# Twelve transfers of v for eight heads in place of 24 for four

## The chip, the cores and the metric

The kernel runs on one core of a Trainium2 chip. A core has five engines that each work through a queue of their own in order: TensorE (PE; its weight loads are shown apart as PEld), VectorE (DVE), ScalarE (ACT), GpSimd (POOL) and SyncE (SP). Sixteen DMA engines move data between the chip's memory and the core's; transfers are issued from the queues of SP, POOL and ACT. The metric is the device time of one execution in microseconds, as the median of several runs.

## The reference

Attention with a decaying state over blocks of 64 rows, and a two-layer network behind it. With B = 4, H = 8, S = 768, D = 64, and a factor `lam` for each head:

```python
for b in range(nb):                       # nb = 768 // 64
    sl = slice(b * block, (b + 1) * block)
    qb, kb, vb = q[:, :, sl], k[:, :, sl], v[:, :, sl]
    intra = einsum('bhic,bhjc->bhij', qb, kb) * Dmask
    intra = einsum('bhij,bhjd->bhid', intra, vb)
    inter = einsum('bhid,bhde->bhie', qb * lam_pow, kv_state)
    out[:, :, sl] = intra + inter
    kv_state = lam_block * kv_state + einsum('bhsd,bhse->bhde', kb * rev_pow, vb)

x = out.transpose(0, 2, 1, 3).reshape(B * S, H * D)      # 3072 x 512
h = x @ w_in                                             # 512 -> 2048
y = (maximum(h, 0) + alpha * minimum(h, 0)) @ w_out      # 2048 -> 512
```

So v is read twice in each block: in the product with the masked scores (`intra`) and in the product that brings the state on (`kv_state`).

## The kernel before

The work is cut into 24 units. Unit n stands for `units[n] = (c, bi, hh)`: c counts six chunks, bi the two batches of a chunk, hh the four heads 0 to 3 or 4 to 7. Chunk c has 256 rows of the sequence (`W`), that is four blocks of 64. Units 2m and 2m + 1 are therefore the two halves of the heads of one batch and the same rows.

A unit's q and k come as fp32 by `load` (L82), which takes eight heads or, with `half`, four, from SP or, with `"G"`, from POOL. `cast` (L257) makes fp16 of them; `turned` (L299, a transposing DMA from SP) or `turn` and `turn_copy` (L309, L323, over PE) bring them with the head's axis on the partitions; `key_decayed` and `decayed` scale them. Its v comes as fp16 by `load_v16` (L268), which POOL issues, since the transfer turns fp32 into fp16 on its way. The 24 transfers go into tiles of `kv_pool`, which has eight for the tag `v16`; the ninth transfer takes the first one's tile, once PE has read it for the last time, and so on.

Then PE works on the unit: `score_products` (L370, in L377), `inter` (L354, in L361) for the part that comes from the state, `intra` (L395, in L402) with v's halves as weights, and `state_products` (L415, in L422; for the first chunks under `state_in`, L466) with v against the decayed k. DVE masks the scores (`masked`, L388) and brings the state on (`states`, L457). `attended` (L431) copies the result as fp16 to `XT[c]`.

The four units of a chunk give one operand of the network: `up` (L493, in L498) for 16 slices of w_in, `relu` on ACT and `prelu` on DVE for the slope, and `down` (L530, in L534) for the first chunk. For later chunks the second product, and for the last two also the first, is done by a scheme with seven products of quarter matrices in place of eight; its sums (`w_sum`, `in_sum`, `g_sum`, `x_sum`) run on DVE and POOL in L573 and L576, and its products on PE in L655 and L780. `load_win` (L97) and `load_wout` (L103) bring the weights, also from POOL and also from fp32 to fp16.

All instructions of an engine are issued in the order of the calls that are written out from L799 to L1866, so the place of a `load_v16` call among the calls that use POOL sets when it is issued, and its place among the calls of POOL and SP what else the DMA engines have been given before it. Waits between engines, on landings and on tiles that are still being read are added from the data that each instruction reads and writes. `gate` (L111) holds SP until a piece of w_in or w_out has landed.

The places that matter below: L820 (unit 1), L833 (0), L836 (2), L841 (3), L889 (4), L941 (5), L1006 and L1007 (7 and 6), L1014 (8), L1103 (9), L1121 (13), L1137 (12), L1161 (10), L1187 (14), L1222 (11), L1261 (19), and from L1329 to L1477 the units 15, 16, 20, 17, 23, 18, 22, 21.

Of the kernel before, what the change touches and what calls it, by code (L numbers as in the profile page):

```python
# [11 lines left out]
def kernel(  # L12
# [19 lines left out]
    fp16 = mybir.dt.float16  # L32
# [4 lines left out]
    B, H, S, D = q.shape  # L37
    assert (B, H, S, D) == (4, 8, 768, 64)
    L = 128
    W = 2 * L  # L40
# [10 lines left out]
    kv_pool = ctx.enter_context(tc.tile_pool(name="kvh", bufs=8))  # L51
# [30 lines left out]
    def load(c, bi, x, half=None, queue="S"):  # L82

        pb, b = c // 2, 2 * (c % 2) + bi
        if (c, bi, x) not in raws:
            raws[c, bi, x] = raw_pool.tile([128, H, 2 * D], fp32, tag=f"{x}raw", name=f"{x}raw")
        heads = ds(0, H) if half is None else ds(4 * half, 4)
        i = "kqv".index(x)
        (nc.gpsimd if queue == "G" else nc.sync).dma_start(
            out=raws[c, bi, x][:, heads, :],  # L90
            in_=(k, q, v)[i][b, heads, ds(pb * W, W), :].rearrange("h (p e) d -> p h (e d)", e=2),
        )
# [4 lines left out]
    def load_win(i):  # L97
        nc.gpsimd.dma_start(
            out=w_in_sb[:, :, ts(i, 512)],
            in_=moe_w_in[:, ts(i, 512)].rearrange("(g p) f -> p g f", p=128),  # L100
        )

    def load_wout(i):  # L103
        nc.gpsimd.dma_start(
            out=w_out_sb[:, ts(i, 4), :],
            in_=moe_w_out[ts(i, 512), :].rearrange("(f p) d -> p f d", p=128),
        )
# [45 lines left out]
    for half in range(2):  # L153
# [7 lines left out]
        out=drop, in0=rel_i, scalar1=0.0, scalar2=-1e30, op0=ALU.is_lt, op1=ALU.mult  # L161
# [42 lines left out]
    def decay_mask(hp):  # L204
        m = dmask[:, hp // 2, :, hp % 2]
        nc.scalar.activation(m, m, AF.Exp)
# [34 lines left out]
    T = {}  # L241
# [3 lines left out]
    def copy_on(eng, out, in_):  # L245
        if eng == "A":
            nc.scalar.activation(out, in_, AF.Copy)  # L247
        elif eng == "V":
            nc.vector.tensor_copy(out=out, in_=in_)
        else:  # L250
            nc.gpsimd.tensor_copy(out=out, in_=in_)  # L251
# [16 lines left out]
    def load_v16(n):  # L268

        c, bi, hh = units[n]  # L270
        v16 = kv_pool.tile([128, 4, 2, D], fp16, tag="v16", name="v16")
        nc.gpsimd.dma_start(  # L272
            out=v16.rearrange("p h e d -> p h (e d)"),
            in_=v[2 * (c % 2) + bi, ds(4 * hh, 4), ds((c // 2) * W, W), :].rearrange("h (p e) d -> p h (e d)", e=2),
        )
        T.setdefault(n, {})["v16"] = v16

    def engine(x):
        return nc.gpsimd if x == "G" else nc.vector
# [29 lines left out]
    def turn(n, xs):  # L309

        t = T[n]
        tp = bank_pool.tile([128, len(xs), 2, 2, L], fp16, tag="bank", name="tp")
        for i, x in enumerate(xs):
            for e in range(2):
                for hp in range(2):
                    nc.tensor.transpose(  # L316
                        tp[:, i, e, hp, :],
                        t["qk16"][:, x, e, ds(2 * hp, 2)].rearrange("p l d -> p (l d)"),
                        ident,
                    )  # L320
        t["tp", xs] = tp

    def turn_copy(n, xs, eng):  # L323

        t = T[n]
        if "qkT" not in t:
            t["qkT"] = qkt_pool.tile([128, 2, 2, 2, L], fp16, tag="qkT", name="qkT")
        tp = t["tp", xs]
        if len(xs) == 1:
            copy_on(eng, t["qkT"][:, xs[0]], tp[:, 0])  # L330
        else:
            copy_on(eng, t["qkT"], tp)
        if xs[0] == 0:
            t["qps"] = tp[:, 0]
# [50 lines left out]
    def masked(n):  # L385
        t = T[n]
        t["sm"] = sm_pool.tile([128, 2, 2, 2, L], fp16, tag="sm", name="sm")
        nc.vector.tensor_tensor(  # L388
            out=t["sm"].rearrange("p a h x j -> p (a h) x j"),
            in0=t["s"].rearrange("p a h x j -> p (a h) x j"),  # L390
            in1=mask_of(units[n][2]),
            op=ALU.mult,
        )
# [37 lines left out]
    def attended(n, *how):  # L431
        co, bo, ho = units[n]
        if co not in XT:
            pool, tag = (raw_pool, "kraw") if co == 5 else (xt_pool, "xT")
            XT[co] = pool.tile([128, NHP, 2, 2, L], fp16, tag=tag, name="xT")
        x = XT[co][:, ds(2 * ho, 2), :, bo, :].rearrange("p h e (a j) -> p a (h e) j", a=2)
        o = acc[:, :, 0:256].rearrange("p a (he j) -> p a he j", j=64)
        if len(how) == 2:
            x, o = x[:, how[0]], o[:, how[0]]
        copy_on(how[-1], x, o)  # L440
# [52 lines left out]
    def up(c, f, bi=None):  # L493
        h = HP[c, f, bi] = bank_of("h_ps")
        n = CH if bi is None else W
        for gi in range(NHP):
            x = XT[c][:, gi]
            nc.tensor.matmul(  # L498
                h[:, 0:n] if bi is None else h[:, 0:n].rearrange("p (e j) -> p e j", e=2),
                lhsT=w_in_sb[:, gi, ts(f, 128)],  # L500
                rhs=x.rearrange("p e b j -> p (e b j)") if bi is None else x[:, :, bi, :],
                start=(gi == 0),
                stop=(gi == NHP - 1),
            )
# [3 lines left out]
    def relu(c, f, bi=None):  # L508
        n = CH if bi is None else W
        m = M[c, f, bi] = m_pool.tile([128, CH], fp32, tag="m", name="m")  # L510
        nc.scalar.activation(m[:, 0:n], HP[c, f, bi][:, 0:n], AF.Relu, scale=-1.0)  # L511

    def prelu(c, f, eng="V"):
        prelu_of(c, f, None, eng)
# [302 lines left out]
    cast(1, "k16", "V")  # L817
    tick(56)
    load(0, 1, "q", 1, "G")
    load_v16(1)  # L820
    decay_mask(1)
    cast(1, "q16", "A")
    mask_logs(3)
# [6 lines left out]
    query_decay(0, 0)  # L830
    load_alpha()
    load(0, 1, "k", 1, "G")
    load_v16(0)  # L833
    turn(1, (0,))
    turn_copy(1, (0,), "V")
    load_v16(2)  # L836
# [1 line left out]
    turn_copy(0, (1,), "V")  # L838
    turn(0, (0,))
    turn_copy(0, (0,), "A")  # L840
    load_v16(3)  # L841
    load_win(1)
    slopes_turn()
    slopes()
# [93 lines left out]
    prelu(0, 15)  # L938
    cast(4, "k16", "G")
    turn(4, (1,))  # L940
    load_v16(5)  # L941
    load_wout(1)
    up(0, 0)
    prelu(0, 14)
# [58 lines left out]
    w_sum(1, 3)  # L1003
    in_sum(1, 2)
    turn(7, (0,))
    load_v16(7)  # L1006
    load_v16(6)  # L1007
    first_state(5)
    down(0, 2, 1)
# [90 lines left out]
    down(0, 1, 2)  # L1100
    down(0, 1, 3)
    attended(6, "A")
    load_v16(9)  # L1103
    up(1, 14)
    cast(10, "q16", "G")
    load(3, 0, "k", None)
# [11 lines left out]
    gpsimd_waits(8)  # L1118
    key_decayed(9)
    masked(8)  # L1120
    load_v16(13)  # L1121
    cast(9, "k16", "A")
    down_copy(0, 1)
    relu(1, 14)
# [9 lines left out]
    prelu(1, 0)  # L1134
    relu(1, 8)
    prelu(1, 8)
    load_v16(12)  # L1137
    relu(1, 11)
    up(1, 7)
    prelu(1, 11)  # L1140
# [17 lines left out]
    masked(9)  # L1158
    prelu(1, 5)
    turned(10)  # L1160
    load_v16(10)  # L1161
    up(1, 12)
    relu(1, 13)
    relu(1, 12)
# [54 lines left out]
    load(4, 0, "k", None)  # L1219
    g_sum(1, 2, 0, 1)  # L1220
    g_sum(1, 3, 0, 0)
    load_v16(11)  # L1222
    second(1, 5, 1)
    g_sum(1, 3, 1, 0)
    states(10, (0, 1))
# [32 lines left out]
    masked(11)  # L1258
    cast(14, "k16", "A")
    cast(16, "k16", "G")  # L1260
    load_v16(19)  # L1261
    second(1, 7, 0)
    second(1, 3, 0)
    second(1, 7, 1)
# [61 lines left out]
    prelu(2, 12)  # L1326
    turned(15)
    second(1, 4, 1)
    load_v16(15)  # L1329
    load_v16(16)  # L1330
    states(14, (0, 1))
    up(2, 13)
    load_v16(20)
    relu(2, 5)
    masked(14)
    second_out(1, 4)
# [9 lines left out]
    prelu(2, 5)  # L1346
    in_sum(2, 2, "G")
    score_products(15)
    load_v16(17)
    prelu(2, 13)  # L1350
    cast(18, "q16", "A")
    turned(17)
# [6 lines left out]
    relu(2, 10)  # L1359
    cast(18, "k16", "A")  # L1360
    key_decayed(19)
    load_v16(23)
    up(2, 9)
    attended(14, "A")
    prelu(2, 10)
# [9 lines left out]
    inter(15)  # L1375
    relu(2, 6)
    load(5, 1, "q")
    load_v16(18)
    relu(2, 9)
    cast(19, "k16", "A")  # L1380
    score_products(16)
# [25 lines left out]
    up(3, 10)  # L1407
    relu(2, 7)
    relu(3, 8)
    attended(16, "A")  # L1410
    up(3, 1)
    prelu(2, 7)
# [28 lines left out]
    cast(20, "q16", "G")  # L1441
    relu(3, 3)
    intra(18)
    load_v16(22)
    score_products(19)
    cast(21, "k16", "A")
    cast(22, "k16", "A")
# [26 lines left out]
    turned(22)  # L1474
    g_sum(2, 3, 1, 1, "G")
    turned(21)
    load_v16(21)  # L1477
    score_products(20)
    state_products(20)
    g_sum(2, 3, 0, 0)  # L1480
# [416 lines left out]
```

## Time and profile before

| | |
|---|---|
| median of three runs | 201.76 us (201.7 to 206.57) |
| the profiled execution | 201.59 us |
| its span | 199.8 us, mean granted TensorE clock 0.999 |
| read from and written to the chip's memory | 27.27 MB and 6.29 MB |
| transfers issued from POOL (q0) | 17,776 packets, 10.23 MB |
| transfers issued from SP (q1) | 41,236 packets, 19.87 MB |
| transfers of v | 24, 128 KB each as they arrive; median 5.5 us from issue to landing |

The span runs from the first to the last instruction of the program; the time of the execution has 1.8 us more around it. The page gives the busy time of each engine, the span in 40 slices of 5 us, the chain of work that ended last, the costliest groups of instructions, and the issues of the DMA queues. In a row of the timeline the columns are the start in us, the time taken in us, the engine, the line, the operation with the names of what it writes and reads, their shapes, and how many instructions the row merges; in brackets stands how long the engine stood idle before and what ended that. An issue on POOL or SP is the making of the transfer's list alone; the data move later, and a transfer has landed when its last byte has been confirmed.

### The profile page before, as it was taken

How to read it: one execution, taken by the hardware profiler on the slowest of the kernel's cores; microseconds unless marked ns; L12 is line 12 of the kernel's file. 1: busy time of each engine (PE TensorE's matmuls, PEld its weight loads, DVE VectorE, ACT ScalarE, POOL GpSimd, SP SyncE). 2: the span in 40 equal slices, each digit the busy share in tenths (PEclk: the TensorE clock that was granted, in tenths of full speed). 3: DMA queues.
4: the chain of work that ended last, by engine and by line, in shares of the span. 5: the costliest groups of instructions: out<-in, count | busy, mean ns of one | idle time of the engine just before them, and what ended most of it. 6: DMA issues, size and time to landing. Idle time of an engine off the chain costs nothing.

```text
span 199.8 us, 5865 instructions
## 1 busy us (share of the span) xinstructions
PE 193.7 (97%) x2351; PEld 129.1 (65%) x2351; DVE 172.7 (86%) x320; ACT 130.9 (66%) x281; POOL 143.0 (72%) x161
## 2 busy tenths in 40 slices
PE   7999999999999999999999999999999999999992
PEld 7875454546545688666557767666666666788891
DVE  6988789999899999899999997899989999895800
ACT  5895775337967898697769589364686986633022
POOL 8999859964999649999999889850575213556700
PEclk9999999999999999999999999999999999999999
DMA  5999999999999989999996925120040001113143
GB/s 165 283 194 216 255 268 232 204 251 295 231 147 265 264 148 242 196 276 130 273 210 147 172 30 152 41 76 0 2 157 3 2 0 54 56 41 117 55 145 118
DMA packets 59199, 30.53 MB, mean 153 GB/s; under 512 B 29652, under 2 KB 57956, under 8 KB 59172
## 3 DMA queue, kind: packets, MB, share of 16 engines
q1 hardware_dynamic: 41236, 19.87, 41.0%
q0 software_dynamic: 17776, 10.23, 34.4%
q8 instruction: 18, 0.29, 0.6%
q14 instruction: 9, 0.07, 0.1%
q10 hardware_dynamic: 160, 0.07, 0.1%
HBM read 27.27 MB, written 6.29 MB: 168 GB/s over the span
## 4 chain that ended last, share of the span: by engine, by line
PE 84%; DVE 10%; ACT 3%; issue 1%; ACTq 0%; DVEq 0%
PE h_ps L498 27%; PE y L655 16%; PE b L655 12%; PE b L780 5%; PE o_ps L534 4%; PE acc L402 4%; PE s L377 3%; PE a L780 3%; PE e L780 3%; DVE sm L388 2%; PE acc L361 2%; PE tp L316 2%; DVE dmask L195 1%; PE acc L422 1%; DVE t L573 1%; ACT xT L247 1%
## 5 line engine op out<-in xcount | busy, mean ns | idle before, releaser
L498 PE MATMUL h_ps<-xT,w_in_sb 128*128 128x512 f16 (+1 forms) x264 | 59.5, 373 | 0.0
L655 PEld LDWEIGHTS <-g 128*128 128x128 f16 x464 | 44.7, 98 | 10.1 <-DVE g L573 0.6
L526 DVE SCALAR_TENSOR_TENSOR g<-m,oma,h_ps 128x512 f16<-128x512 f32 (+1 forms) x66 | 45.7, 725 | 3.6 <-ACT m L511 3.0
L511 ACT ACTIVATE m<-h_ps 128x512 f32<-128x512 f32 (+1 forms) x66 | 37.4, 582 | 15.6 <-PE h_ps L498 14.6
L498 PEld LDWEIGHTS <-w_in_sb 128*128 128x128 f16 x264 | 24.3, 98 | 25.4 <-DMA w_in_sb<-in_moe_w_in_dram 0.9
L388 DVE TENSOR_TENSOR sm<-s,dmask 128x1024 f16<-128x1024 f32 x24 | 29.2, 1217 | 1.7 <-PE s L377 1.7
L655 PE MATMUL y<-w_out_sb,g 128*128 128x256 f16 x224 | 27.9, 273 | 0.3 <-DVE g L573 0.3
L573 POOL TENSOR_TENSOR g<-g 128x512 f16<-128x512 f16 x11 | 13.2, 1204 | 16.3 <-DVE s L576 16.3
L341 POOL TENSOR_TENSOR qdT<-qkT,qdecay 128x512 f16<-128x512 f16 (+1 forms) x20 | 20.9, 1050 | 0.0
L655 PE MATMUL b<-t,g 128*128 128x256 f16 x160 | 19.8, 273 | 0.0
L247 ACT ACTIVATE xT<-acc 128x512 f16<-128x512 f32 x22 | 13.1, 595 | 9.4 <-PE acc L422 5.6
L272 POOL DMA_DIRECT2D v<-in_v_dram x24 | 18.8, 788 | 0.0
L457 DVE SCALAR_TENSOR_TENSOR R<-R,rdecay,acc 128x128 f16<-128x128 f16 x54 | 15.5, 341 | 2.8 <-ACT xT L247 2.2
L573 POOL TENSOR_TENSOR g<-g,g 128x512 f16<-128x512 f16 x12 | 14.3, 1206 | 5.0 <-DVE g L573 2.9
L576 POOL TENSOR_TENSOR s<-g,g 128x512 f16<-128x512 f16 x9 | 10.4, 1156 | 8.4 <-DVE g L526 8.4
L534 PE MATMUL o_ps<-w_out_sb,g 128*128 128x512 f16 x64 | 15.3, 379 | 0.0
L247 ACT ACTIVATE o_sb<-y 128x512 f32<-128x512 f32 (+2 forms) x12 | 6.2, 526 | 13.1 <-PE y L697 7.1
L290 ACT ACTIVATE kdec<-kraw,kdecay 128x64 f16<-128x64 f32 x56 | 14.0, 342 | 0.0
L292 POOL TENSOR_TENSOR kdec<-kraw,kdecay 128x512 f16<-128x512 f32 x13 | 13.6, 1054 | 0.4 <-DVE qdT L341 0.4
L251 POOL CAST qk<-kraw 128x512 f16<-128x512 f32 x10 | 6.5, 654 | 5.0 <-DMA kraw<-in_k_dram 5.0
L377 PE MATMUL s<-qkT 64*64 64x128 f16 x384 | 9.9, 219 | 0.2
L402 PE MATMUL acc<-sm,v 64*64 64x128 f16 x384 | 9.9, 220 | 0.2
(130 smaller groups left out, 369.3 us busy)
## 6 DMA issues: line engine op xcount, KB each, us to landing
out_dram<-o_sb SPq DMA_DIRECT2D x23, 256.0 KB, 2.5
kraw<-in_k_dram SPq DMA_DIRECT2D x7, 512.0 KB, 6.8
qraw<-in_q_dram SPq DMA_DIRECT2D x6, 512.0 KB, 6.1
v<-in_v_dram POOLq DMA_DIRECT2D x24, 128.0 KB, 5.5
w_in_sb<-in_moe_w_in_dram POOLq DMA_DIRECT2D x4, 512.0 KB, 7.8
w_out_sb<-in_moe_w_out_dram POOLq DMA_DIRECT2D x4, 512.0 KB, 9.7
qraw<-in_q_dram POOLq DMA_DIRECT2D x6, 256.0 KB, 6.9
qraw<-in_q_dram SPq DMA_DIRECT2D x6, 256.0 KB, 6.3
```

The lines of the kernel that those rows point to most:

```text
L247: nc.scalar.activation(out, in_, AF.Copy)
L272: nc.gpsimd.dma_start(out=v16.rearrange("p h e d -> p h (e d)"), in_=v[2 * (c % 2) + bi, ds(4 * hh, 4), ds((c // 2) * W, W), :].rearrange( ...
L341: engine(eng).tensor_tensor(out=qdT[:, :, :, p], in0=(t["qps"] if eng == "P" else t["qkT"][:, 0])[:, :, :, p], in1=qdecay[:, hh, :, :, p], ...
L388: nc.vector.tensor_tensor(out=t["sm"].rearrange("p a h x j -> p (a h) x j"), in0=t["s"].rearrange("p a h x j -> p (a h) x j"), in1=mask_of ...
L402: nc.tensor.matmul(ot[a][ds(hl * 64, 64), hp, :], lhsT=t["v16"][p, 2 * hp + hl, e, :], rhs=t["sm"][p, hl, hp, 1 - e, :], start=(2 * pb + a ...
L498: nc.tensor.matmul(h[:, 0:n] if bi is None else h[:, 0:n].rearrange("p (e j) -> p e j", e=2), lhsT=w_in_sb[:, gi, ts(f, 128)], rhs=x.rearr ...
L511: nc.scalar.activation(m[:, 0:n], HP[c, f, bi][:, 0:n], AF.Relu, scale=-1.0)
L526: engine(eng).scalar_tensor_tensor(out=g, in0=m, scalar=oma[:, f : f + 1], in1=h, op0=ALU.mult, op1=ALU.add)
L534: nc.tensor.matmul(O[c, t], lhsT=g_of(c, f)[:, t // 2, t % 2, :], rhs=w_out_sb[:, f, :], start=(f == 0), stop=(f == NF - 1),)
L573: engine(eng).tensor_tensor(out=out, in0=a, in1=b, op=ALU.subtract)
L655: nc.tensor.matmul(Y[c, k][:, ds(b * HALF, HALF)], lhsT=left(c, i, f, b), rhs=right(i, f), start=(f == 0 and b == 0 and i in (1, 5)), stop ...
L780: nc.tensor.matmul(t, lhsT=w, rhs=x, start=(g == 0 and i in (1, 5)), stop=(g == 1), skip_group_check=True)
```

## The change

`load_v16` brings all eight heads of a batch, that is two units, in one transfer into a tile twice as large. There are four such tiles in place of eight, so they take the same room. Both units get their half of the tile as a slice. Each of the twelve calls that stay brings units n and n + 1; the fourth pair before gives its tile. The other calls, their order, the engines and the explicit waits are as before. The diff, with the moved calls and little of what is around them:

```diff
@@ -268,12 +268,13 @@
     def load_v16(n):
 
         c, bi, hh = units[n]
-        v16 = kv_pool.tile([128, 4, 2, D], fp16, tag="v16", name="v16")
+        pair = kv_pool.tile([128, H, 2, D], fp16, tag="v16", name="v16", bufs=4)
         nc.gpsimd.dma_start(
-            out=v16.rearrange("p h e d -> p h (e d)"),
-            in_=v[2 * (c % 2) + bi, ds(4 * hh, 4), ds((c // 2) * W, W), :].rearrange("h (p e) d -> p h (e d)", e=2),
+            out=pair.rearrange("p h e d -> p h (e d)"),
+            in_=v[2 * (c % 2) + bi, :, ds((c // 2) * W, W), :].rearrange("h (p e) d -> p h (e d)", e=2),
         )
-        T.setdefault(n, {})["v16"] = v16
+        for m in (n - hh, n - hh + 1):
+            T.setdefault(m, {})["v16"] = pair[:, ds(4 * (m - n + hh), 4)]
@@ -817,7 +818,7 @@
     load(0, 1, "q", 1, "G")
-    load_v16(1)
+    load_v16(0)
     decay_mask(1)
@@ -830,7 +831,6 @@
     load(0, 1, "k", 1, "G")
-    load_v16(0)
     turn(1, (0,))
     turn_copy(1, (0,), "V")
     load_v16(2)
@@ -838,7 +838,6 @@
     turn_copy(0, (0,), "A")
-    load_v16(3)
     load_win(1)
@@ -938,7 +937,6 @@
     turn(4, (1,))
-    load_v16(5)
     load_wout(1)
@@ -1003,7 +1001,6 @@
     turn(7, (0,))
-    load_v16(7)
     load_v16(6)
@@ -1100,7 +1097,6 @@
     attended(6, "A")
-    load_v16(9)
@@ -1118,7 +1114,7 @@
     masked(8)
-    load_v16(13)
+    load_v16(10)
@@ -1134,7 +1130,6 @@
     prelu(1, 8)
-    load_v16(12)
@@ -1158,7 +1153,7 @@
     turned(10)
-    load_v16(10)
+    load_v16(12)
@@ -1219,7 +1214,6 @@
     g_sum(1, 3, 0, 0)
-    load_v16(11)
@@ -1258,7 +1252,7 @@
     cast(16, "k16", "G")
-    load_v16(19)
+    load_v16(16)
@@ -1326,11 +1320,9 @@
     second(1, 4, 1)
-    load_v16(15)
-    load_v16(16)
+    load_v16(18)
     states(14, (0, 1))
     up(2, 13)
-    load_v16(20)
@@ -1346,7 +1338,6 @@
     score_products(15)
-    load_v16(17)
@@ -1359,7 +1350,7 @@
     key_decayed(19)
-    load_v16(23)
+    load_v16(20)
@@ -1375,7 +1366,6 @@
     load(5, 1, "q")
-    load_v16(18)
@@ -1407,6 +1397,7 @@
     relu(3, 8)
+    load_v16(22)
     attended(16, "A")
@@ -1441,7 +1432,6 @@
     intra(18)
-    load_v16(22)
@@ -1474,7 +1464,6 @@
     turned(21)
-    load_v16(21)
```

The calls for 4 (L889), 8 (L1014) and 14 (L1187) stay where they are and bring 4/5, 8/9 and 14/15.

## The prediction

> **What bounds the kernel now.** I read the page first: the span, the busy shares, the chain and the strip of DMA slices.
>
> ```profile
> span 199.8 us, 5865 instructions
> PE 193.7 (97%) x2351; PEld 129.1 (65%) x2351; DVE 172.7 (86%) x320; ACT 130.9 (66%) x281; POOL 143.0 (72%) x161
> DMA  5999999999999989999996925120040001113143
> PE 84%; DVE 10%; ACT 3%; issue 1%; ACTq 0%; DVEq 0%
> ```
>
> TensorE (PE) works in 97% of the span and 84% of the chain that ended last is PE; GpSimd (POOL), whose queue the change shortens, does not stand in that chain at all. PE takes its instructions in order, so whatever stops it early moves everything behind it. The DMA engines are full (digit 9) from the second slice to about 110 us (slices are 5 us). So the question is less what POOL saves than when each half of v lands against the PE instruction that first needs it.
>
> Next, the waits and POOL's groups kept apart by shape, with the page's list of DMA issues.
>
> ```profile
> PEld L316 <- POOL qk L251: 0.3, 1, 0.3
> PEld L655 <- POOL g L573: 0.2, 1, 0.2
> ...
> POOL g L573 <- DVE s L576: 16.3, 3, 8.1
> ```
> ```profile
> L272 POOL DMA_DIRECT2D v<-in_v_dram x24 | 18.8, 788 | 0.0
> L89 POOL DMA_DIRECT2D qraw<-in_q_dram x6 | 4.6, 761 | 0.6 <-DMA w_in_sb<-in_moe_w_in_dram 0.6
> L98 POOL DMA_DIRECT2D w_in_sb<-in_moe_w_in_dram x4 | 3.1, 767 | 0.0
> ```
> ```profile
> v<-in_v_dram POOLq DMA_DIRECT2D x24, 128.0 KB, 5.5
> w_in_sb<-in_moe_w_in_dram POOLq DMA_DIRECT2D x4, 512.0 KB, 7.8
> ```
>
> PE and its weight loads wait 0.3 + 0.2 = 0.5 us for POOL in the whole run. An issue on POOL costs about 0.78 us whether it brings 128 KB (788 ns) or 512 KB (767 ns), so bytes do not set it. All of these transfers, however, have the same number of pieces by the code: 128 partitions times four (four heads of v or q, four groups of w_in). No row has 128 times eight.
>
> **The change part by part.** *Twelve issues less.* The ends for an issue of eight heads are 0.79 us (one issue, as bytes do not matter) and 2 x 0.79 = 1.58 us (two, if pieces set it). POOL thus saves between 24 x 0.788 - 12 x 0.79 = 9.4 us and nothing. No row lies nearer to either, so I take the middle, 1.2 us an issue and 4.5 us saved. Its worth on the path is near zero: POOL is not in the chain, and its longest wait, 16.3 us, is for VectorE (DVE). If all PE waits for POOL went, that would be the 0.5 us above. Nothing below rests on the issue's price, unless it is far above 1.58 us (a rival).
>
> *The second half of each pair comes earlier, and the first half waits for it.* One transfer signals one landing, so a unit that had its own now waits for both halves. What a half costs in landing time: the view of tile v on POOL, stretch by stretch, gives issue and time to landing.
>
> ```profile
> L272 POOL DMA_DIRECT2D v<-in_v_dram x1: 766/766/766, 5.1 to 5.1; - x1
> DMA to landing us min/median/max: 5.0/5.0/5.0
> ...
> L272 POOL DMA_DIRECT2D v<-in_v_dram x3: 776/791/922, 6.6 to 8.0; - x3
> DMA to landing us min/median/max: 4.8/5.0/6.0
> ...
> L272 POOL DMA_DIRECT2D v<-in_v_dram x1: 780/780/780, 18.7 to 18.7; - x1
> DMA to landing us min/median/max: 8.5/8.5/8.5
> ...
> L272 POOL DMA_DIRECT2D v<-in_v_dram x2: 757/774/792, 36.8 to 37.6; - x2
> DMA to landing us min/median/max: 4.9/4.9/4.9
> ...
> L272 POOL DMA_DIRECT2D v<-in_v_dram x1: 786/786/786, 42.3 to 42.3; - x1
> DMA to landing us min/median/max: 7.7/7.7/7.7
> ...
> L272 POOL DMA_DIRECT2D v<-in_v_dram x3: 747/769/797, 55.4 to 56.9; - x3
> DMA to landing us min/median/max: 4.3/5.6/6.8
> ```
>
> Issued 0.75 us apart, the triple at 6.6 us has its first two landings at 6.6 + 5.0 = 11.6 and 7.3 + 4.8 = 12.1 us: a half costs 0.5 us there. The two at 36.8 and 37.6 land 0.8 us apart. The triple at 55.4 us lands at 55.4 + 4.3 = 59.7, 56.2 + 5.6 = 61.8 and 56.9 + 6.8 = 63.7 us, so a half costs 2 us where loads of the other queue run beside it. These are the ends for the price of a half: 0.5 and 2.0 us.
>
> Now the first uses of v, in PE's timeline, with ACT's cast of k for unit 3 and the row behind it.
>
> ```profile
> 10.85 0.29 PE L422 MATMUL kv<-v,kdec 64*64 64x64 f16 x8
> ...
> 13.75 0.29 PE L422 MATMUL kv<-v,kdec 64*64 64x64 f16 x8
> ...
> 27.52 0.32 PE L422 MATMUL acc<-v,kdec 64*64 64x64 f16 x16
> ...
> 43.45 0.29 PE L422 MATMUL acc<-v,kdec 64*64 64x64 f16 x16
> ...
> 50.51 0.29 PE L422 MATMUL acc<-v,kdec 64*64 64x64 f16 x16
> ...
> 67.90 0.29 PE L422 MATMUL acc<-v,kdec 64*64 64x64 f16 x16
> ...
> 99.29 0.39 PE L402 MATMUL acc<-sm,v 64*64 64x128 f16 x16
> ```
> ```profile
> 11.45 0.62 ACT L247 ACTIVATE qk<-kraw 128x512 f16<-128x512 f32 x1
> 12.04 0.60 ACT L247 ACTIVATE qkT<-tp 128x512 f16<-128x512 f16 x1
> ```
>
> - Pair 0/1 (at the place of unit 1, L820): lands at 5.1 + 5.0 + 0.5 to 0.8 = 10.6 to 10.9 us against 10.85: no wait, or 0.05 us. The load of k for unit 3, issued behind it, moves by the same 0.5 to 0.8 us, which can hold ACT's cast at 11.45 us by some 0.3 us; ACT works without a pause behind that cast, so I put 0.3 us on PE's start of the up products at 17 us.
> - Pair 2/3 (L836): the same bytes are ahead as before, so it lands when the last of the triple did, 8.0 + 6.0 = 14.0 us, against a first use at 13.75: 0.25 us, in the shadow of those 0.3 us.
> - Pair 4/5 (L889): 18.7 + 8.5 = 27.2, plus 0.5 to 0.8, is 27.7 to 28.0 us against 27.52. PE stands up to 0.5 us, of which 0.3 us are the lateness it already has. The k load behind it (0.7 us later) has the next row as its reader, and a late POOL reaches the qdT below.
>
> ```profile
> 28.12 0.61 POOL L251 CAST qk<-kraw 128x512 f16<-128x512 f32 x1 [2.43 <-DMA kraw<-in_k_dram]
> ...
> 33.77 0.68 POOL L341 TENSOR_TENSOR qdT<-qkT,qdecay 128x256 f16<-128x256 f16 x1
> ...
> 41.16 1.16 POOL L573 TENSOR_TENSOR t<-w_out_sb,t 128x512 f16<-128x512 f16 x1 [1.66 <-DMA w_out_sb<-in_moe_w_out_dram]
> 42.25 0.79 POOL L272 DMA_DIRECT2D v<-in_v_dram  x1
> ```
>
> POOL starts that cast when k lands, so it runs 0.7 us late from 28.1 us and its qdT for unit 4 ends near 35.1 us, about 0.6 us behind now. PE reads it in L361 right then, so I count 0.6 us at 35 us. At 41.16 us POOL waits for w_out, whose place in the order of bytes is unchanged (unit 5's half has only moved ahead of it), so POOL is back on time there.
>
> - Pair 6/7 (L1007): it lands as the later of the two did, 37.6 + 4.9 = 42.5 us; unit 7 is first read at 43.45. Hidden.
> - Pair 8/9 (L1014) is the largest term. Unit 8 alone lands at 42.25 + 7.7 = 49.95 us, 0.56 us ahead of its use. With the second half it lands between 50.45 and 51.95. Loads of q and k run beside it, as beside the triple at 55.4 us (2.0 us a half) and less so beside the pair at 36.8 us (0.8 us). I take the middle of these two, 1.4 us: 51.35 us, so PE stands until about 51.4 where it started at 50.51: 0.9 us late. Because landings are fixed by the DMA engines, this is measured from the old time and swallows the 0.6 us; it is not added to it.
> - Pairs 10/11 to 22/23 are issued from 55.4 us on at places that served units read much later; the margin that I rely on is 10/11, landing near 55.4 + 4.3 + 2.0 = 61.7 us against its first reading at 67.90. A pair takes the tile of the fourth pair before it, and POOL would wait if that were still being read. The closest is 22/23, whose place (L1410 in the old numbering) comes behind the row below, at 103.7 us; the last reading of 14/15 is the L402 row at 99.29 us. POOL would have to come 4 us earlier to wait.
>
> ```profile
> 102.60 1.15 POOL L573 TENSOR_TENSOR g<-g 128x512 f16<-128x512 f16 x1
> ```
>
>
> Sum: 0.9 us late at 51 us, and behind it a chain of PE to the end with nothing that gives it back. Twelve landing signals less are worth nothing that a row shows. The profiled execution took 201.59 us (199.8 us of span and 1.8 us around it), 0.17 us under the median of the runs, 201.76 us. So 201.59 + 0.9 = 202.5 us against that execution and 202.7 against the median; I say 202.6.
>
> By the Trainium skill ("DMA: Bandwidth & Descriptors", the section on the anatomy of a GpSimd DMA) a transfer costs about 2.0 us plus bytes over 436 GB/s; its figures would make the second half worth an estimated 131,072 / 436,000 = 0.30 us. By that rule pair 8/9 lands at 50.25 us, ahead of its use, and the first rival below holds; the trace has 0.5 to 2.0 us for such a half, so I give it the smaller chance.
>
> **The rivals.** *Hidden anyway.* If a half costs 0.5 us everywhere, as between 11.6 and 12.1 us, pair 8/9 lands at 50.45, still ahead of 50.51; the late k and pair 4/5 leave about 0.3 us. That gives 201.9 us, with 0 to 0.4 late. Against it: beside other loads the rows show 0.8 and 2.0.
>
> *POOL was worth something.* Issues at 0.79 us free POOL of 9.4 us; the 0.5 us of PE waits go, and DVE, which the chain names for 10%, meets POOL's sums at other moments. That would give up to 1 us, about 201.0 us. Against it: no POOL in the chain.
>
> *A doubled issue costs far more than two.* If it holds POOL for X us (say, until there is room for its descriptors), the two early pairs take 2X in place of four issues, 0.77 + 2.40 = 3.2 us, and POOL's work at 10 us slides onto PE's path with about 0.7 us of room; pair 4/5 adds X - 0.8 - 0.6 more (0.6 us is POOL's idle time by the q row above). At X = 1.58 that is 0 + 0.2 us; at X = 3 it is 2.1 + 1.6 = 3.7 us, and about 0.4 us of other lateness brings it to 4.1. So over 2% (4.0 us) is reached from X = 3 us on: about 206 us. Against it: 0.79 us stands in every row, whatever the size.
>
> **How the numbers follow.** Forecast (half at 0.8 to 2.0 us, so 0.3 to 1.5 us late, and up to 2.2 us if the doubled issue also delays the data by 0.8): 0.62. Hidden: 0.20. POOL worth something: 0.12. Costly issue: 0.05, and 0.01 for a gain over 2% that I have not found. The range goes from 201.3 (most of the gain excluded) to 203.8 us (201.6 + 2.2), which leaves out the costly issue and the better half of the gains, together with some of the forecast's ends. Two per cent is 4.0 us, about what a measurement of this kernel tells from no change; the first three cases lie within it: same 0.94, slower 0.05, faster 0.01.
>
> **What would show it.** Right: PE standing before L422 near 50.5 us until v lands between 50.7 and 52 us, and its later rows shifted by that amount; a short wait before L422 at 27.5 us; POOL's cast of k at about 28.8 us. An issue of v under 1.6 us and PE waits for POOL still under 1 us. Wrong: v of pair 8/9 landing before 50.5 us, PE's rows at 60 us unmoved, or an issue of 3 us; a gain would show as PE rows earlier than now after 60 us, with DVE or POOL ahead of them in the chain.

## The result, and the profile after

The changed kernel took 203.25 us (median of five, 202.97 to 204.27) against 201.76 us before: a ratio of 1.008, interval 1.0053 to 1.0108. It is slower by 1.5 us, less than 2%. The profiled execution took 202.97 us, with a span of 201.2 us against 199.8.

The first fence is the page of the changed kernel: the span, the busy shares, the strip of DMA slices, the chain that ended last, the group of v's issues and its line in the list of DMA issues.

```profile
span 201.2 us, 5854 instructions
PE 193.5 (96%) x2351; PEld 129.4 (64%) x2351; DVE 173.1 (86%) x320; ACT 131.2 (65%) x281; POOL 137.0 (68%) x149
DMA  5999999999999999999999805120040001113143
PE 78%; DMA 7%; DVE 6%; ACT 2%; POOL 2%; issue 1%; ACTq 0%; DVEq 0%; POOLq 0%
L272 POOL DMA_DIRECT2D v<-in_v_dram x12 | 11.1, 925 | 0.0
v<-in_v_dram POOLq DMA_DIRECT2D x12, 256.0 KB, 6.5
```

An issue of eight heads takes 925 ns, so the twelve take 11.1 us where the 24 took 18.8, 7.7 us less. POOL as a whole is busy for 6.0 us less (143.0 to 137.0), so its other work takes 1.7 us more. PE does the same work in 0.2 us less, and yet the span is 1.4 us longer. So PE stands more than before. To find where, I set the start of each PE instruction of the changed kernel against the same instruction before. The lateness is under 0.1 us until 7.7 us, 0.23 us there, 0.75 at 8.7, 1.33 at 14.3, 1.15 from 18.7 on, 0.78 at 47 and 1.13 from 94 on; the last 0.22 of the 1.35 us come at the very end of the span. When the up products start, PE is later than at any time behind them, and neither of the two places of the forecast (28 and 51 us) adds to it.

What happens at 8 us is seen on POOL and DVE. POOL's timeline, first the kernel before, then the changed one (start, time taken, engine, line, operation; xN merges N instructions):

```profile
5.09 0.77 POOL L272 DMA_DIRECT2D v<-in_v_dram  x1
5.83 0.77 POOL L89 DMA_DIRECT2D kraw<-in_k_dram  x1
6.58 2.40 POOL L272 DMA_DIRECT2D v<-in_v_dram  x3
8.96 1.50 POOL L98 DMA_DIRECT2D w_in_sb<-in_moe_w_in_dram  x2
```
```profile
5.11 0.91 POOL L272 DMA_DIRECT2D v<-in_v_dram  x1
5.99 0.78 POOL L89 DMA_DIRECT2D kraw<-in_k_dram  x1
6.74 0.92 POOL L272 DMA_DIRECT2D v<-in_v_dram  x1
7.62 1.54 POOL L98 DMA_DIRECT2D w_in_sb<-in_moe_w_in_dram  x2
```

DVE's timeline of the same microseconds, before and changed: the casts of k of unit 1 and of q of unit 0.

```profile
7.26 0.42 DVE L249 CAST qk<-kraw 128x512 f16<-128x512 f32 x1
...
8.25 0.41 DVE L249 CAST qk<-qraw 128x512 f16<-128x512 f32 x1
```
```profile
7.26 0.65 DVE L249 CAST qk<-kraw 128x512 f16<-128x512 f32 x1
...
8.48 0.94 DVE L249 CAST qk<-qraw 128x512 f16<-128x512 f32 x1
```

And PE's timeline, before (one row) and changed:

```profile
7.73 1.39 PE L316 MATMUL tp<-ident,qk 128*128 128x128 f16 x16
```
```profile
7.97 0.84 PE L317 MATMUL tp<-ident,qk 128*128 128x128 f16 x12 [0.28 <-DVE qk L249]
9.47 0.40 PE L317 MATMUL tp<-ident,qk 128*128 128x128 f16 x4 [0.66 <-DVE qk L249]
...
15.66 0.30 PE L403 MATMUL acc<-sm,v 64*64 64x128 f16 x6 [0.37 <-issue]
```

The issue of pair 2/3 now runs until 7.66 us and the first cast starts in the middle of it: 0.65 us in place of 0.42. The two issues of w_in start at 7.62 us, 1.34 us earlier than before, and the second cast lies beside them: 0.94 us in place of 0.41. PE's transposes of those tiles run as one row of 16 before; now they stand 0.28 and 0.66 us for DVE. The last row is another matter: PE stands in the middle of 16 products that need nothing new ("issue": no wait that the profile shows). The trace's packets offer a reason. A queue of the kind `instruction`, q8, brings 18 pieces of 16 KB in the run; by their number they should be PE's program, since PE and its weight loads are 4702 of the 5854 instructions. One piece starts at 13.28 us, where it started at 11.94 before. That it holds the products at which PE stands is an inference; the other traces bear on it below, under what stays open.

The places where the forecast saw the loss, in the changed kernel: v's landings by stretch, then PE's timeline.

```profile
L272 POOL DMA_DIRECT2D v<-in_v_dram x1: 924/924/924, 19.1 to 19.1; - x1
DMA to landing us min/median/max: 9.1/9.1/9.1
...
L272 POOL DMA_DIRECT2D v<-in_v_dram x1: 937/937/937, 43.0 to 43.0; - x1
DMA to landing us min/median/max: 7.4/7.4/7.4
```
```profile
28.60 0.32 PE L423 MATMUL acc<-v,kdec 64*64 64x64 f16 x16
...
35.58 0.28 PE L362 MATMUL acc<-qdT,R 128*128 128x128 f16 x2
...
51.30 0.29 PE L423 MATMUL acc<-v,kdec 64*64 64x64 f16 x16
```

Pair 4/5 lands at 19.1 + 9.1 = 28.2 us and PE comes for it at 28.60; pair 8/9 lands at 43.0 + 7.4 = 50.4 us and PE comes at 51.30. No row has a wait in brackets. PE is 1.08, 1.07 and 0.79 us behind the old 27.52, 34.51 and 50.51 already when it gets there.

### The profile page after: what moved, and what is told of

It is laid out like the page before. It is cut to its first block, busy times and chain, and to the rows that moved or that the text cites. A ratio compares the mean times of both kernels' runs of the same rounds, so it can differ in the third digit from the quotient of the medians.

```text
span 201.2 us, 5854 instructions
## 1 busy us (share of the span) xinstructions
PE 193.5 (96%) x2351; PEld 129.4 (64%) x2351; DVE 173.1 (86%) x320; ACT 131.2 (65%) x281; POOL 137.0 (68%) x149
## 4 chain that ended last, share of the span: by engine, by line
PE 78%; DMA 7%; DVE 6%; ACT 2%; POOL 2%; issue 1%; ACTq 0%; DVEq 0%; POOLq 0%
PE h_ps L499 24%; PE y L656 16%; PE b L656 10%; DMA qkT<-qk 7%; PE o_ps L535 7%; PE b L781 5%; PE acc L403 3%; PE e L781 3%; PE a L781 3%; PE s L378 3%; PE acc L362 2%; PE tp L317 2%; DVE dmask L195 1%; POOL g L574 1%; POOL qdT L342 1%
## 5 line engine op out<-in xcount | busy, mean ns | idle before, releaser
L574 POOL TENSOR_TENSOR g<-g 128x512 f16<-128x512 f16 x11 | 13.3, 1208 | 16.3 <-DVE s L577 16.3
L574 POOL TENSOR_TENSOR g<-g,g 128x512 f16<-128x512 f16 x12 | 14.3, 1204 | 5.0 <-DVE g L574 2.9
L535 PE MATMUL o_ps<-w_out_sb,g 128*128 128x512 f16 x64 | 15.3, 380 | 0.0
L272 POOL DMA_DIRECT2D v<-in_v_dram x12 | 11.1, 925 | 0.0
```

Of the source, the lines that this page charges most:

```text
L535: nc.tensor.matmul(O[c, t], lhsT=g_of(c, f)[:, t // 2, t % 2, :], rhs=w_out_sb[:, f, :], start=(f == 0), stop=(f == NF - 1),)
L574: engine(eng).tensor_tensor(out=out, in0=a, in1=b, op=ALU.subtract)
```

## The experiments

Two theories were set against each other from here. The first (S in the expectations): the loss is made in the first 10 us, because POOL, ahead of time, meets DVE's casts. Against it (L): the later pairs, by the landings of the forecast or by landings further on, make it. In the kernels that mix the two kinds, `load_half` is the load of four heads as it was, into one half of a pair's tile. "Lateness" is always that of PE against the kernel before, instruction by instruction, in the profiled execution, and so that of one execution each. Two kernels below have the same instructions as the kernel before in their first 55 us (those with only units 10 to 15 and only units 16 to 23 in pairs); they are 0.45 and 0.24 us late at 52 us all the same. So a lateness under some 0.4 us is not told from chance unless a row shows its wait.

**The first four units by four transfers again, the rest in pairs.**

```diff
-    load_v16(0)
+    load_half(1)
...
+    load_half(0)
...
-    load_v16(2)
+    load_half(2)
...
+    load_half(3)
```

> The changed kernel, but units 0 to 3 get their v by four transfers of four heads at the old places; pairs from 4/5 on. Theory S (start): POOL, rid of two issues, makes its two w_in issues while DVE casts k and q of units 1 and 0 at 7.3 and 8.5 us; the casts take 0.65 and 0.94 us in place of 0.42 and 0.41, and that is the loss. Then here the casts are back at 0.41 to 0.42 us, PE's first turn of q of unit 1 starts at 8.7 us as before, and the time is 201.6 to 202.3 us (what is left: about 0.3 us of a wait for a transposing transfer near 95 us, and 0.3 us gained near 45 us). Theory L (landings): v, or k behind it, or the transposes land later because of the pairs from 4/5 on; then the time stays at 202.9 to 203.4 us.

Measured: 203.89 us (202.69 to 205.48), ratio 1.0095, 1.0061 to 1.013. The start is as S said: both casts take 0.42 us and the lateness at 7.7 us is 0.01. The time is not. PE stands at 14.3 us again (0.42), pair 4/5 and the qdT behind it bring the lateness to 0.85 at 35.4 us, and one more step, of 0.8 us, comes at 75 us, where DVE and POOL meet in the sums. DVE's, POOL's and PE's timeline of this kernel there:

```profile
74.22 1.39 DVE L588 TENSOR_TENSOR g<-g,g 128x512 f16<-128x512 f16 x1
```
```profile
74.18 1.15 POOL L588 TENSOR_TENSOR g<-g,g 128x512 f16<-128x512 f16 x1 [0.83 <-PE y L670]
```
```profile
76.80 0.42 PE L417 MATMUL acc<-sm,v 64*64 64x128 f16 x16 [0.73 <-DVE sm L403]
```

POOL's sum started 0.04 us before DVE's, and DVE's took 1.39 us where the same sum before took 0.41; the mask behind it was late, and PE stood 0.73 us for it. DVE's and POOL's rows of the kernel before at this place (POOL's merges three sums):

```profile
73.63 0.41 DVE L573 TENSOR_TENSOR g<-g,g 128x512 f16<-128x512 f16 x1
```
```profile
73.62 3.67 POOL L573 TENSOR_TENSOR g<-g,g 128x512 f16<-128x512 f16 x3 [0.86 <-PE y L655]
```

In all fourteen traces POOL's sum starts first here. Where it leads by 2 to 16 ns (eleven traces, the kernels before and after the change among them), POOL's is the long one, 1.44 us in place of 1.15, and DVE's keeps its 0.41. Where it leads by 40 to 82 ns (this kernel and two below), DVE's takes 1.37 to 1.39 us and PE loses 0.8 us. So a clean start is no cure here: the chain of pair 4/5 shows, and which of the two sums is held goes with some 0.03 us of POOL's start.

**Only the first four units in pairs, the rest as before.** Here the tiles are placed by hand, in the order of the issues. The cut is against the kernel before; the loads that stay single become `load_half` at their places.

```diff
-    load_v16(1)
+    load_v16(0)
...
-    load_v16(0)
...
-    load_v16(3)
...
-    load_v16(4)
+    load_half(4)
```

> The kernel before, but units 0 to 3 get their v by two transfers of eight heads; all the others as before. Theory S: the casts at 7.3 and 8.5 us are long (0.65 and 0.94 us) and the time is 202.6 to 203.4 us. Theory L: 201.6 to 202.0 us.

Measured: 203.32 us (203.18 to 203.46), ratio 1.0068, 1.0056 to 1.008. DVE's timeline:

```profile
7.26 0.64 DVE L249 CAST qk<-kraw 128x512 f16<-128x512 f32 x1
...
8.47 0.93 DVE L249 CAST qk<-qraw 128x512 f16<-128x512 f32 x1
```

The lateness follows the changed kernel's to 0.03 us through the first 47 us: 0.22, 0.73, 1.33, 1.15 and 0.76. That is S, with every later pair taken away. From 117 us on another 0.8 us is added (0.35 at 117.68, 0.24 at 118.56, 0.23 at 135.60) that the changed kernel does not have. It is of the test's own making. POOL's timeline before, POOL's of this kernel, and PE's:

```profile
113.54 0.80 POOL L272 DMA_DIRECT2D v<-in_v_dram  x1
```
```profile
116.85 0.81 POOL L288 DMA_DIRECT2D v<-in_v_dram  x1 [2.22 <-PE s L393]
```
```profile
118.90 1.05 PE L671 MATMUL b<-t,g 128*128 128x256 f16 x8 [0.19 <-POOL g L589]
```

The last load, of unit 21, was put into the half tile of unit 19, which PE reads until then; POOL waits 2.22 us and its sum behind it is late for PE. Before, POOL issued this load without a wait at 113.54 us, ahead of unit 19's last product with v (the L402 row at 115.25 us), so it had another tile, and the tiles are not given strictly in turn. Three kernels below place this load in the same half and carry the same wait; their first 100 us are free of it.

**The issue of w_in held until the second cast is done, and the issue of pair 2/3 held instead.** Both are the changed kernel with one more wait; `gpsimd_waits(0)` makes the transfer that POOL issued last in the order of calls wait for DVE's cast of unit 0's q.

```diff
     load_win(1)
+    gpsimd_waits(0)
```
```diff
     load_v16(2)
+    gpsimd_waits(0)
```

> The changed kernel with one more wait: POOL issues the first w_in transfer only when DVE has finished the cast of q of unit 0. Theory S: that cast is back at about 0.41 us (the one at 7.3 us, beside the issue of pair 2/3, stays near 0.65), PE is 0.25 us late at 9 us in place of 0.75, and the time is 202.0 to 202.7 us. Theory L: nothing changes, 202.9 to 203.4 us.

Measured: 202.64 us (202.13 to 204.54), ratio 1.006, 1.0035 to 1.0086. DVE's and POOL's timeline:

```profile
8.48 0.41 DVE L249 CAST qk<-qraw 128x512 f16<-128x512 f32 x1
```
```profile
9.19 1.50 POOL L98 DMA_DIRECT2D w_in_sb<-in_moe_w_in_dram  x2 [1.53 <-DVE qk L249]
```

With no issue beside it the second cast takes 0.41 us again, while the first keeps its 0.65; the lateness at 9 us is 0.23 in place of 0.75. As S said. The stand at 14 us is smaller (from 0.23 to 0.55), and at 34.5 us the qdT of unit 4, the forecast's chain, brings the lateness from 0.38 to 0.61; from 47 us on 0.41 is left. As a time it is not told from the changed kernel, since the intervals overlap.

> The changed kernel with one more wait, now one issue earlier: POOL issues pair 2/3 only when DVE has finished the cast of q of unit 0 (8.7 us), so that no issue meets the casts at 7.3 and 8.5 us. Theory S (start): both casts take 0.41 to 0.42 us, PE is not late at 9 us; POOL is 0.7 us later with the decayed k and q of units 0 and 2, which PE wants at 14 us, so 0.1 to 0.3 us may come back there; the two steps of pair 4/5 (PE before v at 27.5 us and before qdT of unit 4 at 34.5 us) show, as they did when the first four were single. Time of a good run 201.8 to 202.4 us, median up to 0.8 above. Rival: the late landing of pair 2/3 costs more than the casts did, 203 us or more.

Measured: 204.27 us (203.94 to 206.28), ratio 1.0128, 1.0096 to 1.016. POOL's timeline:

```profile
9.01 0.89 POOL L272 DMA_DIRECT2D v<-in_v_dram  x1 [2.24 <-DVE qk L249]
```

Both casts take 0.42 us, but pair 2/3 is issued 2.3 us later and lands at 14.03 us, and w_in behind it is late too: lateness 0.32 at 9 us, 0.69 at 12.4, 1.49 at 18.7, where PE waits for w_in, and 2.62 at 75, of which 0.81 is DVE's long sum again. Holding the transfers costs more than the casts did, as the rival had it.

**Units 0 to 9 single, pairs from 10/11 on; and units 0 to 5 single, pairs from 6/7 on.** Both are the first kernel of this section with more loads taken back:

```diff
-    load_v16(4)
+    load_half(4)
...
+    load_half(5)
...
-    load_v16(6)
+    load_half(7)
+    load_half(6)
...
-    load_v16(8)
+    load_half(8)
...
+    load_half(9)
```

> The changed kernel, but units 0 to 9 get their v by ten transfers of four heads at the old places; pairs from 10/11 on. Theory S: as with units 0 to 3 alone, within 0.3 us, so 201.6 to 202.3 us. If pairs 4/5 and 8/9 cost something too, it is faster than that kernel by what they cost; if the pairs from 10/11 on cost the 0.35 us near 95 us by landing before the transposes of q and k, that wait stays in both.

> Units 0 to 5 by single transfers at the old places, pairs from 6/7 on. If pair 4/5 is what stopped PE at 27.5 and 34.5 us with the first four single (0.21 us each), both steps are gone here, and 8/9 is the only early pair with little room left (v lands 0.4 to 1.0 us ahead of its reading at 50.5 us): no step there either, or one under 0.3 us. Time of a good run 201.8 to 202.3 us; the median 0.2 to 1.0 above, as with pairs from 10/11 on.

Measured: 202.71 us (201.77 to 203.67), ratio 1.0033, 1.0014 to 1.0052, and 202.53 us (201.94 to 204.21), ratio 1.0036, 1.0016 to 1.0057. The first median is 0.4 us above what was expected. With units 0 to 9 single no lasting step is left at 7.7, 27.5, 34.5 or 50.5 us; the profiled execution (202.03 us, one of the shorter of its twelve) is 0.33 late from 18.7 us on, where PE waits for w_in, and 0.4 at the end. With units 0 to 5 single there is none at 27.5, 34.5 or 50.5 us either: pair 8/9 did not hold PE, which was 0.4 us late there. Its profiled execution, the slowest of its twelve, lost 1.0 us between 60.6 and 63.7 us, where PE waits for DVE's slopes, 0.8 at 75.4 us by DVE's long sum and the mask behind it, and 0.4 at 94 us. The executions of each lie 2 us apart. At 75 us it is a matter of which sum is held, as above; what else tells a short execution from a long one was not traced.

**Only units 10 to 15 in pairs, and only units 16 to 23**, the rest as before, tiles by hand in an order of their own. The cuts are against the kernel before:

```diff
-    load_v16(13)
+    load_v16(10)
...
-    load_v16(12)
...
-    load_v16(10)
+    load_v16(12)
...
-    load_v16(11)
```
```diff
-    load_v16(19)
+    load_v16(16)
...
-    load_v16(16)
+    load_v16(18)
...
-    load_v16(23)
+    load_v16(20)
...
+    load_v16(22)
```

> The kernel before, but units 10 to 15 come as three pairs (issued from 55 to 62 us); all the others single at their old places. With pairs from 10/11 on the runs spread from 201.8 to 203.7 us, where the kernel before spreads 0.8 us. Theory M: the middle pairs cause it, since they bring two units more by 62 us and push the transposes of q and k of units 11 to 14; then the median is 202.3 to 203 us and the spread over 1 us here. Theory late: it is 201.6 to 202.1 us with the spread of the kernel before.

Measured: 201.84 us (201.61 to 203.75; ten of the eleven executions within 202.16), ratio 0.9999, 0.998 to 1.0018. Three pairs in the middle cost nothing and bring nothing that is clear of the interval, though POOL has three issues less: the theory that they make the loss (M) falls, and with it the hope that POOL's time is worth anything there.

> The kernel before, but units 16 to 23 come as four pairs (issued from 80 to 104 us); all the others single at their old places. Theory M: 201.6 to 202.1 us with the spread of the kernel before. Theory late: the median is 202.3 to 203 us and the spread over 1 us.

Measured: 202.37 us (202.05 to 203.04), ratio 1.0024, 1.0012 to 1.0036: half a microsecond. The one large step of the profiled execution, 0.8 us at 112.3 us, starts on ACT. Its timeline:

```profile
111.50 0.63 ACT L247 ACTIVATE qk<-kraw 128x512 f16<-128x512 f32 x1 [1.73 <-DMA kraw<-in_k_dram]
```

ACT waits 1.73 us for a k; its copy of a state's product, DVE's step of the state and PE's L361 are late behind it. The old kernel cast two k's at 108.90 us without a wait. That k landed late is read from the row; that the pairs of v ahead of it were what made it late was not tried by itself, and the changed kernel has no step there.

**The first kernel with pairs again (units 0 to 3 only), made slower on POOL.** If POOL is too early, work that puts it back should bring time. Two transfers of eight numbers that nobody reads are added, one behind each pair's issue:

```diff
+    def small():
+        t = const.tile([H, 1], fp32, name=f"unread{len(SMALL)}")
+        SMALL.append(t)
+        nc.gpsimd.dma_start(out=t, in_=lam.rearrange("(h o) -> h o", o=1))
...
     load_v16(0)
+    small()
...
     load_v16(2)
+    small()
```

> The kernel with only units 0 to 3 in pairs (203.32 us), and after each of the two pair issues one small transfer more from POOL (lam, 32 bytes, into a tile that nobody reads), so that POOL comes to its w_in issues about as late as before the change. Theory S (start: POOL is too early): more work on POOL makes the kernel faster. The casts at 7.3 and 8.5 us are back at 0.41 to 0.42 us, PE is not late at 9 us, and the time is 201.6 to 202.1 us if a small issue takes about 0.6 us. Rival: the pairs themselves (their landing, k of unit 3 behind them, their 0.92 us of issue) cost the 1.4 us; then the time stays at 203.1 to 203.5 us.

Measured: 202.36 us (202.19 to 203.68), ratio 1.003, 1.0012 to 1.0048, against 1.0056 to 1.008 without the two: 0.8 us faster by the ratios, 1.0 by the medians, with two instructions more, and the intervals do not meet. POOL's timeline and DVE's:

```profile
8.15 0.62 POOL L298 DMA_DIRECT2D unread<-in_lam_dram  x1
8.75 1.52 POOL L98 DMA_DIRECT2D w_in_sb<-in_moe_w_in_dram  x2
```
```profile
8.25 0.42 DVE L249 CAST qk<-qraw 128x512 f16<-128x512 f32 x1
```

The w_in issues are back near their old place, both casts take 0.42 us, PE is 0.02 us late at 7.7 us, 0.16 at 15 us and 0.21 early at 47. So PE is 0.97 us ahead of the kernel without the two at 47 us; most of this is the casts (0.73 at 8.7 us), and the stand at 14 us is smaller too (0.16 in place of 0.62). The time missed the expectation by 0.3 us; the profile has 0.8 us from 117 us on (0.36 + 0.24 + 0.21), the test's own wait.

**Only pair 4/5, and only pair 8/9**, the forecast's two landings each by itself with a start as before:

```diff
     load_v16(4)
...
-    load_v16(5)
```
```diff
     load_v16(8)
...
-    load_v16(9)
```

> The kernel before, only units 4 and 5 in a pair. The prediction's own chain, from a start that is not late: PE stands before v of unit 4 (27.5 us) for 0.2 to 0.5 us, and again before qdT of unit 4 (34.5 us), 0.6 us late in all; the time is 202.0 to 202.5 us. Rival: the lateness is taken up near 45 us by DVE's chain, then 201.7 to 202.0 us.

Measured: 203.19 us (202.82 to 203.58), ratio 1.0055, 1.0035 to 1.0076. PE's and POOL's timeline:

```profile
28.02 0.32 PE L437 MATMUL acc<-v,kdec 64*64 64x64 f16 x16
...
35.20 0.27 PE L376 MATMUL acc<-qdT,R 128*128 128x128 f16 x2
```
```profile
28.84 0.61 POOL L251 CAST qk<-kraw 128x512 f16<-128x512 f32 x1 [3.60 <-DMA kraw<-in_k_dram]
```

The pair lands at 27.97 us, PE starts 0.50 us late, POOL's cast 0.72 and the qdT's reader 0.69: the forecast's chain. Of the 0.50, 0.30 was there from 18.7 us on, so the pair's own two steps are 0.2 us each. That it lands later is no chance: a single load of unit 4 lands 8.2 to 8.6 us behind its issue in eight traces, pair 4/5 8.9 to 9.4 us in six. The time is 0.7 us above the expected range, by the wait of unit 21's load, 0.36 + 0.24 + 0.20 us from 117 us on.

> The kernel before, only units 8 and 9 in a pair. The prediction's largest term: v lands at 51.35 us and PE stands 0.9 us before it, 202.4 to 202.9 us. Rival, from the changed kernel's trace (the pair was issued 0.7 us later and landed 0.4 us later than unit 8 alone): the second half costs at most 0.4 us, PE does not stand, or for under 0.2 us, and the time is 201.6 to 202.0 us.

Measured: 203.17 us (202.41 to 204.84), ratio 1.0059, 1.0037 to 1.008. PE's timeline:

```profile
51.14 0.32 PE L437 MATMUL acc<-v,kdec 64*64 64x64 f16 x16 [0.33 <-DMA v<-in_v_dram]
```

The pair lands at 51.09 us where the single load did at 49.95, and PE starts at 51.14, 0.63 us behind the 50.51 of before; 0.13 of this was there already, so the pair's own step is 0.50. In this execution, then, the term of the forecast is there. It need not be in another: a single load of unit 8 lands 5.8 to 8.3 us behind its issue in seven traces, at 48.3 to 50.7 us, and pair 8/9 7.4 to 8.8 us behind its issue in seven others. The old 49.95 is one draw of many, and the rival, that the term is hidden, is not refuted for every execution. The time is 0.3 us above the expected range; here too 0.36 + 0.23 + 0.21 us from 117 us on belong to unit 21's load.

**The changed kernel with the two small transfers.**

```diff
     load_v16(0)
+    small()
...
     load_v16(2)
+    small()
```

> The changed kernel with the same two small transfers. Theory S: the start is as before the change, the waits of pair 4/5 come out (0.4 us in all by the trace with the first four single), and pairs from 16/17 on add 0.2 to 1.5 us that differs from run to run: a good run at 202.0 to 202.6 us, median 202.3 to 203.2. Rival: 203.2 us or more, as the changed kernel.

Measured: 202.77 us (201.91 to 202.92), ratio 1.0031, 1.0016 to 1.0046: its interval lies below that of the changed kernel (1.0053 to 1.0108). So POOL's early start is worth 0.5 us of the 1.5 by the medians and 1.0 us by the ratios. All casts are at 0.42 us, and the lateness at 8.7 us is 0.09. PE still stands at 14 us (0.44 late at 15.3), and with PE nearer to time the qdT shows (0.69 at 34.5); 0.41 is left at 47, 0.9 at 76 and 1.16 at 94 us, so this one execution, among the longer of its twelve, loses the gain again further on. No kernel tried is faster than the one before.

## Why the prediction was right in the time and wrong in the place

The forecast was 202.6 us, slower by less than 2%; 203.25 lies in its range. The loss that it explained is not the one that the changed kernel shows, so the time came out right in good part by luck: the largest term of the sum cost nothing here, and a loss that the sum did not have took its place. By its own signs it was wrong in one: v of pair 8/9 landed before 50.5 us. PE's rows at 60 us did move, by 0.78 us, but not for the reason given.

- *The step that failed* is the worth of POOL's saving: "Its worth on the path is near zero", and "Nothing below rests on the issue's price". The price was well bounded (925 ns, between 0.79 and 1.58), and POOL saves 18.8 - 11.1 = 7.7 us where I had 4.5. But I asked only who waits for POOL, and not what POOL runs beside. An engine that comes earlier costs time where its work lies beside another's: the issue of pair 2/3 lengthened one cast by 0.23 us, the issues of w_in, at 7.62 in place of 8.96 us, another by 0.53 us, and PE was 0.75 us late at 8.7 us. Two kernels with the first pairs alone, one of them with POOL put back by two small transfers, show in the time that POOL's early start costs; the wait ahead of w_in shows in the cast's row that the issue beside it is what lengthens it.
- *Pair 0/1 and 2/3.* Landing 5.1 + 5.7 = 10.8 us as said (10.6 to 10.9). Pair 2/3 landed at 12.8 us, not at 14.0, since it was issued 1.3 us before the place of the old third load. That these loads put 0.3 us on PE at 17 us is not what happened: PE was 1.35 us late there by the casts and by the stand at 14 us.
- *Pair 4/5.* Landing 28.2 us (27.7 to 28.0 said; the issue came at 19.1 in place of 18.7), with no wait, as PE was 1.08 us late. By itself the chain held: 0.50 us at 27.5 (0.30 of it an earlier lateness) and 0.69 at 35 us, where 0.5 (0.3 of it earlier) and 0.6 were said.
- *Pair 8/9*, the largest term: 51.35 us and 0.9 us said, 51.09 and 0.50 alone with a start on time. Against the one landing that the forecast had, the half cost 51.09 - 49.95 = 1.14 us (1.4 said). In the changed kernel the pair landed at 50.4 and cost nothing. What was wrong here is the fixed landing ("landings are fixed by the DMA engines"): the single load lands anywhere from 48.3 to 50.7 us in the traces, and the pair varies by 1.4 us from issue to landing, so whether PE waits is a matter of the execution. The 0.8 and 2.0 us that bounded a half were gaps between landings of loads issued some 0.8 us apart, and so held that spacing too. By the Trainium skill's fit ("DMA: Bandwidth & Descriptors", the anatomy of a GpSimd DMA), which gives an estimated 0.30 us for this half, the term would not exist. The traces say more: 8.1 us from issue to landing on the mean of seven pairs against 6.8 on that of seven single loads.
- *Pairs from 10/11 on, "hidden".* Right for 10 to 15 (0.9999). For 16 to 23 v itself is on time, but the late pairs alone cost 0.5 us, in the profiled execution by way of a k that ACT waits for; the changed kernel has a 0.35 us step at 94 us, where PE's weight loads wait for a transposed q or k. I had looked at v's own readers alone.
- *The rivals.* A costly issue is refuted at 925 ns. "POOL was worth something" had the mechanism (POOL meets DVE at other moments) and the wrong sign. "Hidden anyway" was right of pair 8/9 in the changed kernel and wrong in its sum.
- *That the terms do not add.* Alone, the first pairs leave PE 0.76 us late at 47 us, pair 4/5 0.70 at 35 us and pair 8/9 0.63 at 51 us, together 2.1, or 1.7 without the 0.30 and 0.13 that were there ahead of the last two; the changed kernel is 0.79 late at 51 us and 1.13 at the end. A landing costs nothing to an engine that is late already (28.2 us against 28.60 for pair 4/5). I used this rule ("swallows the 0.6 us") but with one term missing at its head.

What stays open: PE's stand at 14 us, 0.6 us in the changed kernel and with the first pairs alone. In the fourteen traces it goes with the start of q8's piece. Where the piece starts at 10.90 to 12.06 us, there is no stand (four traces); at 12.18 to 12.25 us it is 0 to 0.17 us (four), at 12.39 to 12.50 us 0.32 to 0.44 us (four), and at 13.28 and 13.29 us 0.60 and 0.62 us; PE goes on 2.2 to 2.5 us behind the piece's start wherever it has stood. With POOL's first issues at their old places the start lies between 11.94 and 12.50 us (eight traces), so a stand of up to 0.44 us comes by chance. It is at 13.3 us in the two kernels where w_in comes early, at 12.40 with w_in held, at 10.90 with pair 2/3 held too, and at 12.25 and 12.48 us with the small transfers. So the fetch is late either by POOL's transfers ahead of it or by PE's own lateness at that time, 0.73 to 0.75 us in just those two kernels. The 10.90, with PE 0.32 us late, speaks for the transfers; no test set the two apart.

## What to carry to other kernels

When an edit frees time on an engine, list what that engine will then run earlier, and beside which instructions of the engine that shares something with it; "nobody waits for it" bounds only the gain. A late engine hides later losses, so price each term with the path on time, and expect that mending the first uncovers the next. The landing in one trace is one draw: a term that rests on half a microsecond of room needs the landings of several executions. A test that places tiles by hand has to be read for its own waits before its time is used.

## What the runs showed of the hardware

- The issue of a transfer by POOL costs by its pieces, weakly: 0.56 and 0.62 us for eight pieces, 0.77 for 512, 925 ns for 1024; bytes do not matter (788 ns for 128 KB and 767 for 512 KB, both of 512 pieces). The numbers of pieces are counted from the code.
- A cast from fp32 to fp16 of 128x512 on DVE takes 0.41 us alone and 0.65 to 0.94 beside issues on POOL; with nothing but a wait of POOL added it is 0.41 again. It is not simply a question of being beside one: in the kernel before, the cast at 8.25 us lies beside the third v issue of the row at 6.58, keeps its 0.41, and an issue of that row takes 922 ns in place of 776. The Trainium skill ("SBUF — State Buffer", "Who interferes with whom") says that DVE and GpSimd share a port pair, that a cast can take it, and that the one that comes first holds it for its whole instruction. The trace agrees that either of the two can be the one held (the cast by 0.53 us, the issue by 0.15); which of them, it does not show to follow from the rows' starts. For the two sums near 74 us POOL's row starts first in all fourteen traces: with a lead of 40 to 82 ns DVE's is held (1.37 to 1.39 us in place of 0.41), as the rule has it; with a lead of 2 to 16 ns POOL's is, though first by its row (1.44 us in place of 1.15).
- What a second half of 128 KB in one transfer costs beside other loads: at 19 to 28 us the landing comes 8.9 to 9.4 us behind the issue in place of 8.2 to 8.6 (six traces against eight), 0.7 us on the mean. At 42 to 51 us it is 7.4 to 8.8 us in place of 5.8 to 8.3 (seven against seven), 1.3 us on the mean, and the scatter of one and the same load is larger than the effect.
